# Loading the last 64 rows of w_down as 128 half rows on all partitions, in a one-core attention and FFN decode kernel

## The chip, the core and the metric

The kernel runs on one core of a Trainium2 chip. The metric is device time in microseconds (us). The core has a matmul engine (PE), a vector engine (DVE), an activation engine (ACT), a general engine (POOL), a sequencer that issues transfers (SP), and 16 DMA engines that move data from device memory (HBM) into on-chip memory (SBUF), which has 128 partitions. PE accumulates in PSUM.

## The reference

One token goes through layer norm, then through attention over a cache of 32,768 positions (32 heads of 128) and through a SwiGLU feed-forward block. Both results are added to the input.

```
xn = layernorm(x)                                  # 1 x 640
q  = xn @ wq ; p = softmax(q k^T / sqrt(128)) ; o = p v        # 32 heads, k and v: 32768 x 128 each, bf16
A  = o @ wo                                        # wo: 4096 x 640
B  = (silu(xn @ w_gate) * (xn @ w_up)) @ w_down    # w_gate, w_up: 640 x 1728 ; w_down: 1728 x 640
out = x + A + B
```

The hidden size 1728 is 13 x 128 + 64. These last 64 rows of `w_down` are what the change is about.

## The kernel before

All big loads go through one ring of three slots and are issued by SP, in order: `wq`, then keys and values head by head, then the FFN weights in one slot, then `w_o` in another. Below is the part of SP's program for the FFN and `w_o` (D = 640, F = 1728, FM = 13, FL = 64, NCD = 5).

```
wd = flat[:, d0:d0 + FB * D].rearrange("p (j d) -> p j d", j=FB)
# ... SP:
e.dma_start(wg, B_w_gate.rearrange("(p c) n -> p (c n)", c=NCD)).then_inc(s_ffn[0], 16)
e.dma_start(wu, B_w_up.rearrange("(p c) n -> p (c n)", c=NCD)).then_inc(s_ffn[1], 16)
e.dma_start(flat[:, d0:d0 + FM * D], B_w_down[0:FM * 128, :].rearrange(
    "(p j) n -> p (j n)", j=FM)).then_inc(s_ffn[2], 16)
e.dma_start(wd[0:FL, FM, :], B_w_down[FM * 128:F, :]).then_inc(s_ffn[2], 16)   # 64 rows, 64 partitions
# ... then w_o in six pieces of 8, 8, 8, 5, 2 and 1 rows per partition
```

PE computes gate and up as columns of 128 hidden values, the fourteenth column with 64; DVE and ACT apply the activation; PE multiplies by `w_down` and `w_o` into one accumulator.

```
for j in range(FB):                                   # gate, then up
    n = 128 if j < FM else FL
    for c in range(NCD):
        mm = t.matmul(ffn[0:n, i * FB + j:i * FB + j + 1], lhsT=hidden(w, c, j), rhs=xn[:, c:c + 1], ...)
# ... down:
for j in range(FB):
    n = 128 if j < FM else FL
    for c in range(NCD):
        t.matmul(acc[:, c:c + 1], lhsT=wd_v[0:n, j, c, :], rhs=hcol[0:n, j:j + 1], ...)
# ... DVE: every FFN step twice, for 128 partitions x 13 columns and for 64 partitions x 1 column
```

## Time and profile before

| | before |
|---|---|
| median of the runs | 1288.67 us |
| span of the profiled run | 1286.8 us |
| DMA, mean over the span | 431 GB/s |
| PE, DVE, ACT busy | 81%, 52%, 4% |

The page of the kernel before gives the busy time of each engine and, in 40 equal slices of the span, the busy share of the DMA engines in tenths and their rate:

```profile
span 1286.8 us, 9861 instructions
...
PE 1044.2 (81%) x5153; PEld 261.3 (20%) x3234; DVE 670.3 (52%) x409; ACT 52.2 (4%) x140; POOL 2.5 (0%) x17
...
DMA  9999999999999999999999999999999999999998
GB/s 422 426 424 449 426 430 441 430 434 428 440 428 432 444 428 432 440 430 434 428 440 428 432 444 428 432 440 428 434 428 442 428 432 444 428 432 440 428 418 358
...
```

The DMA row is 9, which means 90% or more, in 39 of 40 slices. PE and DVE have idle time. So the kernel lasts as long as its DMA queue.

The chain of waits of the same run, in order of time (start in us, duration, what), is followed back from the last instruction:

```profile
...
1253.62 29.08 DMA ring<-in_A_wo_dram
...
1282.75 1.49 PE ps L402 x40
...
1284.36 0.17 DVE outb L592
...
1284.88 0.28 DVE orow L594
```

The last 800 KB piece of `w_o` lands 29.08 us after its issue, at 1282.70 us; 40 matmuls and the finish follow. The timeline of the same run (start, duration, engine, operation, and in brackets the idle time before and what ended it) shows whether PE has slack before that:

```profile
...
1274.31 2.10 PE L392 MATMUL ps<-hcol,ring 128*128 128x1 bf16 x70 [1.49 <-DVE hcol L586]
...
1276.34 2.58 PE L402 MATMUL ps<-ot,ring 128*128 128x1 bf16 x80
...
1280.77 1.45 PE L402 MATMUL ps<-ot,ring 128*128 128x1 bf16 x40 [1.84 <-DMA ring<-in_A_wo_dram]
...
1282.75 1.47 PE L402 MATMUL ps<-ot,ring 128*128 128x1 bf16 x40 [0.53 <-DMA ring<-in_A_wo_dram]
...
```

L392 is down, L402 is the product with `w_o`. PE stands idle for 1.84 and 0.53 us until `w_o` pieces land. Work that is moved about on PE before this point does not move the end.

The list of issues by size gives the median time from issue to landing, last on the line:

```profile
...
ring<-in_A_wo_dram SPq DMA_DIRECT2D x3, 1280.0 KB, 25.0
...
ring<-in_A_wo_dram SPq DMA_DIRECT2D x1, 800.0 KB, 29.1
...
ring<-in_A_wo_dram SPq DMA_DIRECT2D x1, 160.0 KB, 28.9
ring<-in_B_w_down_dram SPq DMA_DIRECT2D x1, 80.0 KB, 32.6
...
```

All of them wait most of these 25 to 33 us in the queue: at 424 GB/s, 1280 KB are only 3.1 us. The 80 KB line is the 64-row load: 1239.0 us (its issue in the timeline) + 32.6 = 1271.6 us. Now the table of stretches of the same run, 3 us each (stretch, its length, busy time of each engine and instruction count, granted PE clock, DMA busy share, GB/s):

```profile
...
core 0: us, PE busy (x) PEld busy (x) DVE busy (x) ACT busy (x) POOL busy (x), PEclk, DMA share, GB/s
1266.00:1269.00 3.00, 2.62 (x42) 2.59 (x43) 0.00 (x0) 0.20 (x1) 0.00 (x0) 0.50 1.08 432
1269.00:1272.00 3.00, 3.00 (x53) 3.00 (x53) 0.00 (x0) 0.00 (x0) 0.00 (x0) 0.50 0.93 325
1272.00:1275.00 3.00, 1.51 (x39) 1.44 (x39) 0.93 (x8) 0.23 (x2) 0.00 (x0) 0.50 1.00 420
1275.00:1278.00 3.00, 2.87 (x101) 2.76 (x99) 0.00 (x0) 0.00 (x0) 0.00 (x0) 0.50 1.02 427
...
```

The DMA busy share stays near 1 (0.93 to 1.08), but the rate is 325 GB/s in the stretch in which the 64 rows are served, against 420 to 432 around it. The engines are busy and yet move a quarter less.

The raw packet records say which packets these are. For the same run (start in us on the record's own clock, whose zero lies 11.1 us before the span's start; duration; bytes), when the first of the 64 rows are served:

```
1279.725 0.792 16640
1279.834 0.542 10240
1279.903 0.812 16640
1280.054 0.606 10240
```

Before and after this stretch a packet of 16,640 B takes 0.62 us and one of 10,240 B 0.386 us. The 64 packets of 1280 B themselves mostly take 55 ns (76 ns at most), as do those of the last `w_o` piece. So the transfer looks harmless in its own record; its neighbours are slowed. Strung together by start and duration, the packets of this run form 16 sequences, as many as there are DMA engines, and every sequence has slowed packets in this stretch: 59 packets in all (16,640 B over 0.68 us, 10,240 B over 0.43 us), two to five in each sequence.

### The profile page before, as it was taken

The numbers are of one execution on the slowest core, as the hardware profiler recorded it, in microseconds if no ns is written. First come the engines' busy times: TensorE is split into PE (matmuls) and PEld (weight loads), VectorE is DVE, ScalarE is ACT, GpSimd is POOL, SyncE is SP. The second block draws the span as 40 slices with busy tenths as digits, with TensorE's granted clock in tenths as the row PEclk, the third lists the DMA queues.
The fourth block names the chain that finished last, engine by engine and source line by source line (L and its number), as shares of the span: only waits on it lengthen the run. The fifth ranks groups of instructions, "written<-read, shape, count | busy, mean of one in ns | idle before, by whom it ended". The sixth has DMA issues, their size and how long they took to land.

```text
span 1286.8 us, 9861 instructions
## 1 busy us (share of the span) xinstructions
PE 1044.2 (81%) x5153; PEld 261.3 (20%) x3234; DVE 670.3 (52%) x409; ACT 52.2 (4%) x140; POOL 2.5 (0%) x17
## 2 busy tenths in 40 slices
PE   4599778789777888778798777798777798778797
PEld 1011112221112221112221112221112221112227
DVE  0855665445664446664446664446664446654440
ACT  2000000000000000000000000000000000000000
POOL 0000000000000000000000000000000000000000
PEclk9799888898888998888898888998888998888995
DMA  9999999999999999999999999999999999999998
GB/s 422 426 424 449 426 430 441 430 434 428 440 428 432 444 428 432 440 430 434 428 440 428 432 444 428 432 440 428 434 428 442 428 432 444 428 432 440 428 418 358
DMA packets 11192, 554.17 MB, mean 431 GB/s; under 512 B 1259, under 2 KB 1452, under 8 KB 1708
## 3 DMA queue, kind: packets, MB, share of 16 engines
q1 hardware_dynamic: 11178, 554.00, 99.7%
q8 instruction: 9, 0.15, 0.0%
q14 instruction: 3, 0.02, 0.0%
q10 hardware_dynamic: 2, 0.00, 0.0%
HBM read 553.99 MB, written 0.00 MB: 431 GB/s over the span
## 4 chain that ended last, share of the span: by engine, by line
DMA 53%; PE 30%; DVE 11%; issue 6%; SPq 0%; DVEq 0%
DMA ring<-in_A_k_cache_dram 51%; PE ps L315 17%; PE ps L283 11%; DVE ring L532 10%; DMA ring<-in_A_wo_dram 2%; PE ps L302 1%; PE ps L357 0%; PE ps L351 0%; PE ps L345 0%; PE ps L402 0%; SPq L227 0%; DVEq L532 0%; DVE sc L538 0%; DVE pmax L544 0%; SPq L203 0%
## 5 line engine op out<-in xcount | busy, mean ns | idle before, releaser
L532 DVE TENSOR_TENSOR ring<-ring,qb 128x8192 bf16<-128x8192 bf16 x128 | 557.8, 4420 | 315.6 <-DMA ring<-in_A_k_cache_dram 315.6
L283 PE MATMUL ps<-ring,ident 128*128 128x512 bf16 x1920 | 500.0, 419 | 0.0
L315 PE MATMUL ps<-ring,P 128*4 128x512 bf16 x1984 | 443.3, 379 | 0.0
L302 PE MATMUL ps<-ring,ident 128*128 128x512 bf16 x128 | 55.9, 437 | 217.8 <-DVE ring L532 217.6
L315 PEld LDWEIGHTS ps<-ring,P 128*4 128x4 bf16 x1984 | 163.4, 85 | 237.8
L302 PEld LDWEIGHTS ps<-ring,ident 128*128 128x128 bf16 x128 | 12.6, 99 | 616.9 <-DVE ring L532 343.6
L538 DVE TENSOR_REDUCE sc<-ps 128x64 f32<-128x512 f32 x128 | 82.2, 683 | 63.5 <-PE ps L283 63.5
L550 DVE TENSOR_SCALAR negb<-ps 128x1 f32<-128x1 f32 x32 | 5.1, 158 | 108.4 <-PE ps L357 108.4
L455 ACT ACTIVATE P<-sc,negb 128x256 bf16<-128x256 f32 x32 | 16.2, 507 | 956.5 <-DVE negb L550 956.5
L547 DVE TENSOR_REDUCE m<-ps 1x1 f32<-1x128 f32 x32 | 8.9, 278 | 85.2 <-PE ps L351 85.2
L337 PEld LDWEIGHTS ps<-identf,o 4*128 4x128 f32 x248 | 30.3, 188 | 13.1 <-issue 13.1
L337 PE MATMUL ps<-identf,o 4*128 4x1 f32 x248 | 32.9, 250 | 0.0
L345 PEld LDWEIGHTS ps<-rsum,ones 128*128 128x128 f32 x64 | 12.1, 190 | 99.9 <-issue 99.0
L446 ACT ACTIVATE o<-ps,rzb 4x512 f32<-4x512 f32 x31 | 21.0, 678 | 6.2 <-PE ps L315 6.2
L275 PE MATMUL ps<-ring 128*128 128x512 bf16 x39 | 11.3, 458 | 11.2 <-DMA ring<-in_A_wq_dram 11.2
L451 ACT ACTIVATE ocol<-ps 128x1 f32 (+1 forms) x31 | 5.4, 173 | 222.0 <-PE ps L337 222.0
L544 DVE TENSOR_REDUCE pmax<-sc 128x1 f32<-128x256 f32 x32 | 13.4, 420 | 0.0
L351 PE MATMUL ps<-identf,pmax 128*1 128x128 f32 x64 | 12.2, 273 | 1.2 <-DVE pmax L544 1.2
L357 PE MATMUL ps<-m,ones 1*128 1x1 f32 x64 | 12.1, 256 | 0.4 <-DVE m L547 0.4
L357 PEld LDWEIGHTS ps<-m,ones 1*128 1x128 f32 x64 | 9.4, 182 | 14.2 <-issue 13.5
L381 PE MATMUL ps<-xn,ring 128*128 128x1 bf16 (+1 forms) x140 | 8.9, 198 | 1.0 <-issue 1.0
L520 DVE RECIPROCAL rzb<-ps 128x1 f32<-128x1 f32 x32 | 5.0, 158 | 8.1 <-PE ps L345 8.1
(62 smaller groups left out, 81.1 us busy)
## 6 DMA issues: line engine op xcount, KB each, us to landing
ring<-in_A_wq_dram SPq DMA_DIRECT2D x1, 5120.0 KB, 15.4
ring<-in_A_v_cache_dram SPq DMA_DIRECT2D x1, 4096.0 KB, 31.8
ring<-in_A_wo_dram SPq DMA_DIRECT2D x3, 1280.0 KB, 25.0
ring<-in_B_w_gate_dram SPq DMA_DIRECT2D x1, 2160.0 KB, 23.0
ring<-in_B_w_up_dram SPq DMA_DIRECT2D x1, 2160.0 KB, 27.7
ring<-in_B_w_down_dram SPq DMA_DIRECT2D x1, 2080.0 KB, 31.8
ring<-in_A_v_cache_dram SPq DMA_DIRECT2D x1, 2048.0 KB, 36.4
ring<-in_A_v_cache_dram SPq DMA_DIRECT2D x2, 1024.0 KB, 39.4
```

The costliest lines, as they stand in the source:

```text
L283: return t.add_instruction(mybir.InstMatmult(start_tensor_calc=False, stop_tensor_calc=stop, tile_size=(128, 128), tile_position=(0, 0), l ...
L302: t.matmul(ob, lhsT=ident[:, :], rhs=src, start=True, stop=False)
L315: mm = t.matmul(O, lhsT=P[:, h % PR, j:j + W], rhs=ring[:, s, j * DH:(j + W) * DH], start=(j == 0), stop=(j + W == NJ))
L337: mm = t.matmul(fold_ps, lhsT=o4[:, m * DH:(m + 1) * DH], rhs=identf[0:W, m:m + 1], start=(m == 0), stop=(m == W - 1))
L345: t.matmul(misc[:, 129:130], lhsT=ones[:, :], rhs=rsum[:, h % SR:h % SR + 1], start=True, stop=True).then_inc(s_z, 1)
L351: t.matmul(misc[0:1, 0:128], lhsT=pmax[:, h % SR:h % SR + 1], rhs=identf[:, :], start=True, stop=True).then_inc(s_t, 1)
L357: t.matmul(misc[:, 128:129], lhsT=ones[0:1, :], rhs=m1[0:1, h % SR:h % SR + 1], start=True, stop=True).then_inc(s_b, 1)
L446: a.activation(out=o4[:, :], in_=O, func=ACTF.Copy, scale=rzb[0:W, h % SR:h % SR + 1]).then_inc(s_o4, 1)
L455: a.activation(out=P[:, h % PR, :], in_=sc[:, :], func=ACTF.Exp, bias=negb[:, h % SR:h % SR + 1], scale=c_scale, accum_out=rsum[:, h % SR: ...
L532: v.tensor_tensor(out=kh, in0=kh, in1=q[:, None, :].to_broadcast([128, HF, DH]), op=ALU.mult).then_inc(s_mul, 1)
L538: v.tensor_reduce(out=sc[:, i * HF:(i + 1) * HF], in_=bank[i].rearrange("p (j e) -> p j e", e=G), axis=AX.X, op=ALU.add).then_inc(s_red, 1)
L544: v.tensor_reduce(out=pmax[:, h % SR:h % SR + 1], in_=sc[:, :], axis=AX.X, op=ALU.max).then_inc(s_max, 1)
```

## The change

The 64 rows become 128 half rows of 320 elements: row f lies on partitions 2f and 2f+1. For this, partitions 2f and 2f+1 both need hidden value f, so DVE copies the last 64 columns of gate and up with every column doubled, PE computes all 128 outputs, and the product is masked by the parity of the partition into two columns, one per half of the output. The intent is a load that uses all partitions, and a simpler set of FFN steps, for a little more work on DVE. The diff, cut to its core:

```diff
-        wd = flat[:, d0:d0 + FB * D].rearrange("p (j d) -> p j d", j=FB)
+        wd = flat[:, d0:d0 + FM * D].rearrange("p (j d) -> p j d", j=FM)
+        wdr = flat[:, d0 + FM * D:d0 + FM * D + D // 2]
...
-                        e.dma_start(wd[0:FL, FM, :], B_w_down[FM * 128:F, :]).then_inc(s_ffn[2], 16)
+                        e.dma_start(wdr, B_w_down[FM * 128:F, :].rearrange(
+                            "f (t n) -> (f t) n", t=2)).then_inc(s_ffn[2], 16)
...
+                    for half in range(2):                                  # PE, down, after columns 0..12
+                        a, b = half * (D // 2), (half + 1) * (D // 2)
+                        for c in range(a // 128, (b + 127) // 128):
+                            m0, m1 = max(a, c * 128), min(b, c * 128 + 128)
+                            t.matmul(acc[m0 - c * 128:m1 - c * 128, c:c + 1], lhsT=wdr[:, m0 - a:m1 - a],
+                                     rhs=hcol[:, FM + half:FM + half + 1],
+                                     start=False, stop=False, skip_group_check=True)
...
+                def twice(i):                                              # DVE
+                    v.wait_ge(s_ffn[i], 16)
+                    v.tensor_copy(out=wt[i].rearrange("p c (f t) -> p c f t", t=2),
+                                  in_=(wg_v, wu_v)[i][:, :, FM * 128:F][:, :, :, None].to_broadcast(
+                                      [128, NCD, FL, 2])).then_inc(s_twice, 1)
...
+                v.tensor_scalar(out=hcol[:, FM:FM + 2], in0=par[:, :], scalar1=sg[:, 0, FM:FB],
+                                scalar2=ffn[:, FB + FM:2 * FB], op0=ALU.mult, op1=ALU.mult).then_inc(s_fd, 1)
```

ACT's two exponentials become one, and DVE's eight FFN steps become four, the mask of parities (`par`) and this masked product.

More of the change, by code (lines that the diff above doesn't have):

```diff
@@ L98, in bass_parallel_sum__gqa_block_cached__swiglu_ffn__decode_kernel @@
         ot = sbt("ot", [128, OC], BF16)
-        hcol = sbt("hcol", [128, FB], BF16)
+        hcol = sbt("hcol", [128, FB + 1], BF16)
+        par = sbt("par", [128, 2], F32)
         sg = sbt("sg", [128, 2, FB], F32)
@@ L131, in bass_parallel_sum__gqa_block_cached__swiglu_ffn__decode_kernel @@
         s_att, s_fin = sem("att"), sem("fin")
+        s_twice = sem("twice")
         s_xr, s_or = sem("xr"), sem("orow")
@@ L147, in bass_parallel_sum__gqa_block_cached__swiglu_ffn__decode_kernel @@
         d0 = f0 + 2 * NCD * F
-        wd = flat[:, d0:d0 + FB * D].rearrange("p (j d) -> p j d", j=FB)
-        assert 2 * NCD * F + FB * D <= CE
+        wd = flat[:, d0:d0 + FM * D].rearrange("p (j d) -> p j d", j=FM)
+        wdr = flat[:, d0 + FM * D:d0 + FM * D + D // 2]
+        assert 2 * NCD * F + FM * D + D // 2 <= CE and 2 * FL == 128 and D % 2 == 0
         wg_v = wg.rearrange("p (c n) -> p c n", c=NCD)
@@ L152, in bass_parallel_sum__gqa_block_cached__swiglu_ffn__decode_kernel, with hidden @@
         wd_v = wd.rearrange("p j (c m) -> p j c m", c=NCD)
-        def hidden(w, c, j):
+        u0 = d0 + FM * D + D // 2
+        wt = [flat[:, u0 + i * NCD * 128:u0 + (i + 1) * NCD * 128].rearrange("p (c m) -> p c m", c=NCD)
+              for i in range(2)]
+        assert u0 + 2 * NCD * 128 <= f0 + CE
+        def hidden(i, c, j):
+            w = (wg_v, wu_v)[i]
             if j < FM:
                 return w[:, c, 0:FM * 128].rearrange("p (m j) -> p m j", j=FM)[:, :, j]
-            return w[:, c, FM * 128:F]
+            return wt[i][:, c, :]
         wo = flat[:, WO_S * CE:WO_S * CE + OC * D]
@@ L376, in hidden_part @@
                     t.wait_ge(s_ffn[i], 16)
-                    w = (wg_v, wu_v)[i]
                     for j in range(FB):
-                        n = 128 if j < FM else FL
+                        if j == FM:
+                            t.wait_ge(s_twice, i + 1)
                         for c in range(NCD):
-                            mm = t.matmul(ffn[0:n, i * FB + j:i * FB + j + 1], lhsT=hidden(w, c, j),
+                            mm = t.matmul(ffn[:, i * FB + j:i * FB + j + 1], lhsT=hidden(i, c, j),
                                           rhs=xn[:, c:c + 1], start=(c == 0), stop=(c == NCD - 1))
@@ L386, in down @@
                     t.wait_ge(s_ffn[2], 32)
-                    t.wait_ge(s_fd, 8)
-                    first = True
-                    for j in range(FB):
-                        n = 128 if j < FM else FL
+                    t.wait_ge(s_fd, 6)
+                    for j in range(FM):
                         for c in range(NCD):
-                            t.matmul(acc[:, c:c + 1], lhsT=wd_v[0:n, j, c, :], rhs=hcol[0:n, j:j + 1],
-                                     start=first, stop=False, skip_group_check=True)
-                            first = False
+                            t.matmul(acc[:, c:c + 1], lhsT=wd_v[:, j, c, :], rhs=hcol[:, j:j + 1],
+                                     start=(j == 0 and c == 0), stop=False, skip_group_check=True)
+                    for half in range(2):
[5 more added lines that the diff above has]
+                                     start=False, stop=False, skip_group_check=True)
                 def project():
@@ L478, in act @@
                 a.wait_ge(s_f, 1)
-                a.activation(out=sg[:, 0, 0:FB - 1], in_=ffn[:, 0:FB - 1], func=ACTF.Exp,
-                             scale=-1.0).then_inc(s_fa, 1)
-                a.activation(out=sg[0:FL, 0, FB - 1:FB], in_=ffn[0:FL, FB - 1:FB], func=ACTF.Exp,
-                             scale=-1.0).then_inc(s_fa, 1)
+                a.activation(out=sg[:, 0, :], in_=ffn[:, 0:FB], func=ACTF.Exp, scale=-1.0).then_inc(s_fa, 1)
             @block.vector
@@ L562, in dve @@
                 rz(H - 1)
+                def twice(i):
[3 more added lines that the diff above has]
+                                      [128, NCD, FL, 2])).then_inc(s_twice, 1)
+                twice(0)
                 h = H - 1
@@ L571, in dve @@
                                 in1=blk[:, None, :].to_broadcast([128, H, RB]), op=ALU.mult).then_inc(s_ob, 1)
-                v.wait_ge(s_fa, 2)
-                pieces = [(slice(0, 128), slice(0, FM)), (slice(0, FL), slice(FM, FB))]
-                n = 0
-                for stage in range(4):
-                    for p, f in pieces:
-                        fu = slice(FB + f.start, FB + f.stop)
-                        if stage == 0:
-                            ins = v.tensor_scalar(out=sg[p, 0, f], in0=sg[p, 0, f], scalar1=1.0, scalar2=None,
-                                                  op0=ALU.add)
-                        elif stage == 1:
-                            ins = v.reciprocal(out=sg[p, 1, f], in_=sg[p, 0, f])
-                        elif stage == 2:
-                            ins = v.tensor_tensor(out=sg[p, 0, f], in0=sg[p, 1, f], in1=ffn[p, f], op=ALU.mult)
-                        else:
-                            ins = v.tensor_tensor(out=hcol[p, f], in0=sg[p, 0, f], in1=ffn[p, fu], op=ALU.mult)
-                        ins.then_inc(s_fd, 1)
-                        n += 1
-                    v.wait_ge(s_fd, n)
+                twice(1)
+                v.tensor_reduce(out=par[:, :], in_=ident[:, :].rearrange("p (f t) -> p t f", t=2),
+                                axis=AX.X, op=ALU.add).then_inc(s_fd, 1)
+                v.wait_ge(s_fa, 1)
+                v.tensor_scalar(out=sg[:, 0, :], in0=sg[:, 0, :], scalar1=1.0, scalar2=None,
+                                op0=ALU.add).then_inc(s_fd, 1)
+                v.wait_ge(s_fd, 2)
+                v.reciprocal(out=sg[:, 1, :], in_=sg[:, 0, :]).then_inc(s_fd, 1)
+                v.wait_ge(s_fd, 3)
+                v.tensor_tensor(out=sg[:, 0, :], in0=sg[:, 1, :], in1=ffn[:, 0:FB], op=ALU.mult).then_inc(s_fd, 1)
+                v.wait_ge(s_fd, 4)
+                v.tensor_tensor(out=hcol[:, 0:FM], in0=sg[:, 0, 0:FM], in1=ffn[:, FB:FB + FM],
+                                op=ALU.mult).then_inc(s_fd, 1)
+                v.tensor_scalar(out=hcol[:, FM:FM + 2], in0=par[:, :], scalar1=sg[:, 0, FM:FB],
+                                scalar2=ffn[:, FB + FM:2 * FB], op0=ALU.mult, op1=ALU.mult).then_inc(s_fd, 1)
                 v.wait_ge(s_xr, 1)
```

## The prediction

> **What bounds the kernel now.** DMA, from end to end. The page's slice row shows the 16 DMA engines 90% or more busy in 39 of 40 slices, and its DMA line a mean of 431 GB/s; PE is busy 81%, DVE 52%. The timeline of the last 30 us shows the same for the stage that the change touches: PE is through gate, up and down by 1276.3 us, then stands idle for w_o pieces (0.2, 1.9 and 0.6 us before three groups of its matmuls). The chain of waits ends in a w_o transfer of 29 us, its matmuls, and about 1 us of finish. The queue is served in order: gate, up, down, the 64 last rows, w_o. What counts is when w_o's last byte lands.
>
> **What the change removes.** The 64-row transfer is only 80 KB, 0.19 us at 430 GB/s. But the table of stretches shows the DMA rate falling while it is served: 420 GB/s in 1272-1275 us and 427 in 1275-1278, but 325 in 1269-1272, around its landing at 1239.0 + 32.6 = 1271.6 us. Single packet records agree: its 64 packets of 1280 B take 55 ns each[...], and in those 2.5 us the neighbours' packets slow down (16,640 B from 0.62 to 0.81 us, 10,240 B from 0.386 to 0.54-0.61 us). The 1280 B packets of the last w_o piece, over 128 partitions, do not do this. The summed shortfall is 0.5 to 0.7 us of the whole queue. [...]
>
> **What it adds.** DMA: 128 packets of 640 B, eight an engine; from 55, 102, 244 and 386 ns for 1280 to 10,240 B I estimate 31 ns each, about 0.02 us more per engine. DVE: two copies of 640 elements, estimated at 0.4 to 0.8 us each (the 128x640 broadcast copy near the start took 0.82 us). The first fits between gate's landing (about 1260.7) and 1263.0; the second follows 1265.7, before PE reaches column 14 (about 1272). PE: as many hidden matmuls, 71 instead of 70 in down. ACT one instruction for two, DVE six FFN steps for eight: the 1.5 us gap before down shrinks by some 0.3 us. All this lies before PE's 2.7 us of idle time, so none of it moves the end.
>
> **Critical path.** Only the DMA dip is on it. If it goes altogether, the end comes 0.5 us or more earlier[...]. I expect 0.5 us, 0.04%.
>
> **Predicted time:** 1288.2 us, 80% range 1287.4 to 1289.0. Faster by over 2%: 0.005; within 2%: 0.985; slower by over 2%: 0.01.
>
> **What would show it.** Right: 1269-1272 us holds 400 GB/s or more; w_o pieces land about 0.5 us sooner after issue; PE still ends with waits for w_o; DVE copies under 0.9 us that no one waits for; PE's gap before down near 1.2 us. Wrong: the dip stays[...]; PE waits at the last gate or up column; the last w_o matmuls no longer wait for DMA.
>
> **What would make it wrong.** 640 B packets disturbing neighbours as much; instruction fetches (16 KB, about 1.1 us on one DMA engine) falling on an engine that finishes last[...]; run-to-run steps of 0.5 us, as large as the effect.

The forecast's sum is one term: 0.5 us off the 1288.67 us measured before, which gives the 1288.2 us. That is the low end of the shortfall of 0.5 to 0.7 us in the DMA rate, which the trace shows. "Eight an engine" is 128 packets over 16 engines, a mean; no record names the engine of a packet. "Served in order" rests on the landings: gate at 1260.7 us, up at 1265.7, down at 1270.3, the 64 rows at 1271.6, the pieces of `w_o` after them. An instruction fetch of 16 KB takes 0.99 to 1.13 us in the packet records of the kernel before.

## The result and the profile after

The kernel after takes 1288.09 us (median of 4 runs, 1288.06 to 1288.20), the kernel before 1288.67 us in the same rounds (1288.64 to 1289.19): 0.58 us less, 0.05%. The measured ratio is 0.9995 with a 95% interval of 0.9977 to 1.0012. Ratios are computed as the mean time of one kernel's runs over that of the other's of the same rounds, so they are not quite the ratio of the medians quoted. The interval is wide beside the effect, but the runs are not: all 4 runs after lie below all runs before, by 0.44 us or more. The experiments below rest on such gaps and on the DMA rate in the profile.

The page of the kernel after:

```profile
span 1286.2 us, 9862 instructions
...
PE 1042.2 (81%) x5154; PEld 261.0 (20%) x3235; DVE 672.2 (52%) x409; ACT 52.2 (4%) x139; POOL 2.5 (0%) x17
...
DMA  9999999999999999999999999999999999999998
GB/s 422 426 424 447 429 428 437 436 428 430 444 428 432 442 430 428 428 446 426 432 444 428 430 434 438 428 430 444 428 432 438 432 430 428 444 428 432 444 411 365
...
```

Nothing stands out at this resolution; only the span is 0.6 us shorter. The chain of waits:

```profile
...
1253.85 28.33 DMA ring<-in_A_wo_dram
...
1282.23 1.46 PE ps L416 x40
...
1283.78 0.17 DVE outb L608
...
1284.30 0.28 DVE orow L610
```

The 800 KB piece was issued 0.23 us later than before (1253.85 against 1253.62), took 28.33 instead of 29.08 us, and so landed 0.52 us sooner, at 1282.18 us. What follows it is as long as before, within 0.06 us. The list of issues says the same of every piece of `w_o`, 0.7 to 0.8 us less from issue to landing:

```profile
...
ring<-in_A_wo_dram SPq DMA_DIRECT2D x3, 1280.0 KB, 24.2
...
ring<-in_A_wo_dram SPq DMA_DIRECT2D x1, 800.0 KB, 28.3
...
ring<-in_A_wo_dram SPq DMA_DIRECT2D x1, 160.0 KB, 28.2
ring<-in_B_w_down_dram SPq DMA_DIRECT2D x1, 80.0 KB, 31.7
...
```

The table of stretches shows where this comes from:

```profile
...
1266.00:1269.00 3.00, 2.25 (x41) 2.25 (x42) 0.82 (x2) 0.20 (x1) 0.00 (x0) 0.50 1.03 436
1269.00:1272.00 3.00, 3.00 (x53) 3.00 (x53) 0.00 (x0) 0.00 (x0) 0.00 (x0) 0.50 1.00 406
1272.00:1275.00 3.00, 1.54 (x48) 1.48 (x48) 0.96 (x5) 0.18 (x1) 0.00 (x0) 0.50 0.98 413
1275.00:1278.00 3.00, 3.00 (x112) 2.97 (x109) 0.00 (x0) 0.00 (x0) 0.00 (x0) 0.50 1.01 427
...
```

In 1269-1272 us the rate is now 406 GB/s instead of 325; 81 GB/s over 3 us is 243 KB, or 0.57 us of the queue at 424 GB/s. That is as much as the whole gain. In the packet records of this stretch the 10,240 B packets stay at 0.385 to 0.394 us (but for one of 0.88 us; the kernel before has one too), and the 640 B packets take 32 ns. The timeline of the added and moved work:

```profile
...
1260.69 0.82 DVE L577 COPY ring<-ring 128x640 bf16<-128x640 bf16 x1 [6.69 <-DMA ring<-in_B_w_gate_dram]
...
1265.81 0.82 DVE L577 COPY ring<-ring 128x640 bf16<-128x640 bf16 x1 [2.34 <-DMA ring<-in_B_w_up_dram]
...
1274.11 1.87 PE L400 MATMUL ps<-hcol,ring 128*128 128x1 bf16 x65 [1.46 <-DVE hcol L604]
...
1280.38 1.40 PE L416 MATMUL ps<-ot,ring 128*128 128x1 bf16 x40 [1.92 <-DMA ring<-in_A_wo_dram]
...
1282.23 1.44 PE L416 MATMUL ps<-ot,ring 128*128 128x1 bf16 x40 [0.46 <-DMA ring<-in_A_wo_dram]
...
```

The two copies take 0.82 us each, and no instruction waits for either. Down (L400) is held for 1.46 us before it starts, against 1.49 us before, and PE still waits for `w_o` at the end (L416).

A measure used below is the *loss* of a profiled run: the sum over half microseconds, from 1277 to 1287 us on the record's clock (to 1289 for the run with 320 KB), of how far the DMA rate in the packet records (each packet's bytes spread evenly over its duration) falls short of 424 GB/s, expressed in us of queue time. It is 0.58 us before and 0.04 us after. It comes from one profiled run of each kernel.

### The profile page after: what moved, and what is told of

It is laid out like the page before. It is cut to its first block, busy times and chain, and to the rows that moved or that the text cites. A ratio compares the mean times of both kernels' runs of the same rounds, so it can differ in the third digit from the quotient of the medians.

```text
span 1286.2 us, 9862 instructions
## 1 busy us (share of the span) xinstructions
PE 1042.2 (81%) x5154; PEld 261.0 (20%) x3235; DVE 672.2 (52%) x409; ACT 52.2 (4%) x139; POOL 2.5 (0%) x17
## 4 chain that ended last, share of the span: by engine, by line
DMA 53%; PE 29%; DVE 12%; issue 5%; SPq 0%; DVEq 0%
DMA ring<-in_A_k_cache_dram 51%; PE ps L325 17%; DVE ring L543 12%; PE ps L293 10%; DMA ring<-in_A_wo_dram 2%; PE ps L312 1%; PE ps L367 0%; PE ps L361 0%; PE ps L355 0%; PE ps L416 0%; SPq L237 0%; DVEq L543 0%; DVE sc L549 0%; DVE pmax L555 0%; SPq L212 0%
## 5 line engine op out<-in xcount | busy, mean ns | idle before, releaser
L391 PE MATMUL ps<-xn,ring 128*128 128x1 bf16 x140 | 8.4, 196 | 1.6 <-issue 1.6
```

## The experiments

Theory A, which the prediction favoured: the whole gain is the vanished dip in the DMA rate. Rival B: the shorter steps on ACT and DVE. Twelve runs were made, all with 5 timed rounds beside the kernel before, in four groups, each group on another chip; the kernel before had medians of 1288.73, 1288.81, 1288.86 and 1288.62 us in them. Differences below are to the kernel before of the same group.

### 1. The load alone, and the arithmetic alone

The kernel before, with the new load only. The arithmetic then reads wrong values:

```diff
-e.dma_start(wd[0:FL, FM, :], B_w_down[FM * 128:F, :]).then_inc(s_ffn[2], 16)
+e.dma_start(flat[:, d0 + FM * D:d0 + FM * D + D // 2], B_w_down[FM * 128:F, :].rearrange(
+    "f (t n) -> (f t) n", t=2)).then_inc(s_ffn[2], 16)
```

> The kernel before with only the transfer of the change: the 64 rows come as 128 half rows on all partitions, the arithmetic stays as before and so reads wrong values (wrong on purpose). Theory A (the dip in the DMA rate while 64 rows go to 64 partitions is the whole gain): the dip goes, about 1288.1 us, as the kernel after. Rival B (the gain comes from the shorter FFN steps on ACT and DVE): the time stays at about 1288.7 us.

Measured: 1288.16 us, 0.57 less than before, loss 0.05 us. The result was wrong, as meant. The stretch of the dip in its table of stretches:

```profile
...
1269.00:1272.00 3.00, 3.00 (x53) 3.00 (x53) 0.00 (x0) 0.20 (x1) 0.00 (x0) 0.50 1.02 415
...
```

The other half of the square: the kernel after, with the old load. Half of the partitions then multiply with leftover data:

```diff
-e.dma_start(wdr, B_w_down[FM * 128:F, :].rearrange("f (t n) -> (f t) n", t=2)).then_inc(s_ffn[2], 16)
+e.dma_start(flat[0:FL, d0 + FM * D:d0 + FM * D + D], B_w_down[FM * 128:F, :]).then_inc(s_ffn[2], 16)
-        u0 = d0 + FM * D + D // 2
+        u0 = d0 + FM * D + D
```

> The kernel after with the old transfer: 64 full rows to partitions 0..63, all added arithmetic kept (wrong on purpose, since the second half of the partitions holds other data). Theory A: the dip is back, about 1288.7 us, as the kernel before, and the added copies cost nothing. Rival B: about 1288.1 us. If the copies cost something that the load hides, this is over 1288.8 us.

Measured: 1288.66 us, 0.07 less than before and within its scatter (1288.52 to 1288.84), loss 0.60 us; wrong, as meant. The same stretch:

```profile
...
1269.00:1272.00 3.00, 3.00 (x54) 3.00 (x53) 0.00 (x0) 0.00 (x0) 0.00 (x0) 0.50 0.90 319
...
```

The load alone gives the gain (0.57 of 0.58 us) and removes the dip; the arithmetic alone gives nothing and keeps it. Rival B is out.

### 2. The same bytes once more, in both forms

Could any 80 KB from one small region of HBM, or any run of short packets, make the dip? Both runs add to the kernel after a second copy of the 64 rows, unused, right behind the first (`last` is `B_w_down[FM * 128:F, :]`, `e0` a free place in the slot). Only the form differs:

```diff
+e.dma_start(flat[:, e0:e0 + D // 2], last.rearrange("f (t n) -> (f t) n", t=2)).then_inc(s_x2, 16)   # x128
+e.dma_start(flat[0:64, e0:e0 + D], last).then_inc(s_x2, 16)                                          # x64
```

> The kernel after with a second, unused copy of the same 80 KB as 128 half rows, right behind the first. Theory A: only its bytes cost: 8 packets of 32 ns an engine, so +0.2 to 0.3 us over the kernel after (1288.3 to 1288.4 us), no dip. Theory C (any 80 KB read from one contiguous stretch of HBM, or any short packets, disturb the queue): +0.6 us or more and a dip.

> The kernel after with a second, unused copy of the same 80 KB as 64 full rows on partitions 0..63, right behind the half rows. Same bytes and same source as the run with the half rows twice. Theory A: a dip as in the kernel before, +0.7 to 0.9 us over the kernel after (1288.8 to 1289.0 us). Theory C: the same time as with the half rows twice.

Measured: 1288.41 us for half rows twice (loss 0.07), 1289.08 us with 64 full rows (loss 0.57). The stretch of each, half rows first:

```profile
...
1269.00:1272.00 3.00, 3.00 (x56) 3.00 (x54) 0.00 (x0) 0.00 (x0) 0.00 (x0) 0.50 1.01 404
...
```

```profile
...
1269.00:1272.00 3.00, 3.00 (x53) 3.00 (x53) 0.00 (x0) 0.00 (x0) 0.00 (x0) 0.50 1.00 337
...
```

Same source, same bytes, same place in the queue: 0.67 us apart. The bytes alone cost about 0.3 us over the kernel after. It is the destination or the packet size, not the source.

### 3. Packet size, and how many partitions

Four more forms of the extra 80 KB (the edits are cut to the transfers). "One packet per engine" is 16 packets over 16 engines, a mean:

```diff
+e.dma_start(flat[0:64, e0:e0 + 800].rearrange("p (t n) -> p t n", t=2)[:, :, 0:D // 2],             # x64half
+            last.rearrange("f (t n) -> f t n", t=2)).then_inc(s_x2, 16)
+e.dma_start(flat[0:32, e0:e0 + 2 * D], last.rearrange("(p r) n -> p (r n)", r=2))...                 # x32
+e.dma_start(flat[0:16, e0:e0 + 4 * D], last.rearrange("(p r) n -> p (r n)", r=4))...                 # x16
+e.dma_start(flat[0:32, e0:e0 + D], last[0:32, :])... ; e.dma_start(flat[64:96, e0:e0 + D], last[32:64, :])...   # x32x2
```

> The kernel after with an extra, unused 80 KB as in the run with 64 extra rows, but each row as two packets of 640 B, so that only the 64 partitions are left of it and the packet size is that of the half rows. Theory A1 (the number of partitions[...] makes the dip): as with 64 full rows, 1288.8 to 1289.3 us, with the dip. Theory R (the packet size makes it): as with half rows on all partitions, 1288.3 to 1288.5 us, no dip.

> Extra, unused 80 KB on partitions 0..31 as 2560 B packets. [...] as with 64 partitions, 1288.8 to 1289.3 us. If the number of partitions counts by itself (half as many): the dip cost doubles from 0.67 to about 1.3 us, near 1289.7 us. If longer packets cure it: 1288.4 us.

> Extra, unused 80 KB on partitions 0..15, one 5120 B packet per engine. [...] near 1290.4 us, and surely over 1289.6 us. [...] near 1289.0 us or less.

> Extra, unused 80 KB as two transfers of 32 rows each, one to partitions 0..31 and one to 64..95: the same rows and packets as with 64 rows[...]. [...] no dip, 1288.4 to 1288.6 us. If it is what all engines do at the moment: a dip as with 64 rows, 1288.9 to 1289.3 us.

| extra 80 KB | packets | us | to before | loss, us |
|---|---|---|---|---|
| partitions 0..127 (section 2) | 640 B | 1288.41 | -0.32 | 0.07 |
| 0..63 (section 2) | 1280 B | 1289.08 | +0.35 | 0.57 |
| 0..63, two packets a row | 640 B | 1289.06 | +0.25 | 0.67 |
| 0..31 | 2560 B | 1288.82 | +0.01 | 0.62 |
| 0..15 | 5120 B | 1289.04 | +0.23 | 0.65 |
| 0..31, then 64..95 | 1280 B | 1288.74 | -0.07 | 0.33 |

The same stretch of these four, in the order of the table (packets of 640 B, 0..31, 0..15, two transfers):

```profile
...
1269.00:1272.00 3.00, 3.00 (x54) 3.00 (x52) 0.00 (x0) 0.00 (x0) 0.00 (x0) 0.50 1.00 325
...
```

```profile
...
1269.00:1272.00 3.00, 3.00 (x53) 3.00 (x53) 0.00 (x0) 0.00 (x0) 0.00 (x0) 0.50 0.97 328
...
```

```profile
...
1269.00:1272.00 3.00, 3.00 (x53) 3.00 (x52) 0.00 (x0) 0.00 (x0) 0.00 (x0) 0.50 0.97 317
...
```

```profile
...
1269.00:1272.00 3.00, 3.00 (x53) 3.00 (x53) 0.00 (x0) 0.00 (x0) 0.00 (x0) 0.50 0.98 358
...
```

Packet size is out: 640 B packets on 64 partitions make the full dip, and packets of 2560 and 5120 B do not cure it. The expectation for 16 partitions failed: about 1290.4 us was expected, and 1289.04 us was measured, as in its other branch (near 1289.0 us or less). The same 80 KB lost 0.57 us on 64 partitions, 0.62 us on 32 and 0.65 us on 16: within the lower half the number of partitions hardly changes the loss of these 80 KB. The run on 0..31 has the full loss in the records, yet a median time 0.2 to 0.3 us below those of the other one-sided runs in the table. The profiled executions, from which the losses come, do not differ so: 1288.86 us on 0..31 against 1288.85, 1288.91 and 1288.91 us. The gap lies in executions without a profile and is not explained.

What 0..15, 0..31 and 0..63 have in common is that they lie in the lower half of the partitions. Two transfers of 32 rows, one in each half, lost 0.33 us, about half, and their time, 1288.74 us, lies between the two expectations (1288.4 to 1288.6 us without a dip, 1288.9 to 1289.3 us with one). Why it is about half is not shown.

### 4. Another window of 64 partitions

The single transfers to fewer than 128 partitions so far all began at partition 0. Two more runs move the window of 64 partitions and keep rows and packets: 32..95 has 32 partitions in each half, 64..127 is the upper half. A third writes four times the bytes to 0..63. Theory H is that the dip goes by which partitions are written, so that 32..95 has none and 64..127 has one.

```diff
+e.dma_start(flat[32:96, e0:e0 + D], last).then_inc(s_x2, 16)      # x64mid
+e.dma_start(flat[64:128, e0:e0 + D], last).then_inc(s_x2, 16)     # x64hi
+e.dma_start(flat[0:64, e0:e0 + 4 * D], B_w_down[F - 256:F, :].rearrange("(p r) n -> p (r n)", r=4)).then_inc(s_x2, 16)   # x64d4
```

> Extra, unused 80 KB as 64 full rows on partitions 32..95. [...] Theory H[...]: no dip, 1288.3 to 1288.5 us as with half rows. Theory N (fewer than 128 partitions is enough, whichever): dip, 1288.8 to 1289.2 us.

> Extra, unused 80 KB as 64 full rows on partitions 64..127[...]. Theory H and theory N: dip as on 0..63, 1288.8 to 1289.2 us. If it is special to partitions 0..63, which hold something else: no dip, 1288.4 us.

> Extra, unused 320 KB on partitions 0..63: four times the bytes, one transfer, rows of 5120 B. The bytes alone cost 0.77 us at 424 GB/s over the kernel after. Theory D (the loss goes by bytes, 0.6 us per 80 KB): 2.4 us more, near 1291.3 us. Theory M (the whole queue is slowed as long as any one engine is in such a transfer; the engines pass it over 2.2 us, so 0.6 us longer engine time each makes the slow stretch only 1.3 times as long): loss 0.8 us, near 1289.7 us.

Measured: 1288.59 us on 32..95 (0.27 less than before, loss 0.05); 1288.96 us on 64..127 (0.10 more, loss 0.54); 1292.59 us with 320 KB on 0..63 (3.73 more, loss 2.03). Their stretches, in this order:

```profile
...
1269.00:1272.00 3.00, 3.00 (x54) 3.00 (x53) 0.00 (x0) 0.00 (x0) 0.00 (x0) 0.50 0.99 402
...
```

```profile
...
1269.00:1272.00 3.00, 3.00 (x53) 3.00 (x52) 0.00 (x0) 0.00 (x0) 0.00 (x0) 0.50 1.00 341
...
```

```profile
...
1269.00:1272.00 3.00, 3.00 (x53) 3.00 (x52) 0.00 (x0) 0.00 (x0) 0.00 (x0) 0.50 1.02 218
1272.00:1275.00 3.00, 1.54 (x51) 1.48 (x51) 0.96 (x5) 0.18 (x1) 0.00 (x0) 0.50 0.97 328
...
```

The run on 32..95 decides. Its transfer has 64 partitions, 1280 B packets, and the same source and bytes as the one to 0..63; it has no dip (402 GB/s in the stretch, loss 0.05 us), and in its packet records no sequence has a slowed packet. (Its time is 0.09 us over the range expected, that of the run on 0..63 0.08 us.) So "fewer than 128 partitions" is not the cause; it matters which partitions are written. The upper half alone is about as bad as the lower (0.54 against 0.57 us). So the pattern in these runs is: a transfer of 80 KB that lies in one half of the partitions loses 0.54 to 0.67 us, one that lies evenly in both 0.04 to 0.07 us, and two one-sided transfers, one for each half, lose 0.33 us together. What in the chip makes this pattern is not shown: no run tells one mechanism from another.

With four times the bytes the rate falls to 218 GB/s, about half of the usual, for a whole stretch. Why it is half is not shown. Theory M of the expectation (a fixed slow stretch, about 1289.7 us) is out; theory D (by bytes) gave 1291.3 us, and even that was 1.3 us too low. Of the 4.5 us over the kernel after, by the medians, 0.77 us are bytes and 2.03 us are loss in the records; 1.7 us are left. The profiled run was one of the two quickest of the five (1292.03 us), which accounts for 0.56 us of it. The packet records show where the other 1.2 us lie: one of the sequences of packets finishes late. Its last eight packets of `w_o` are alone in the record and end at 1286.88 us of the span, against 1282.91 us for the last packet in the kernel after, 4.0 us later, while the point at which 300 KB are still to come is only 2.8 us later. Why it is late is not known.

### 5. A kernel made from this

If it is enough to write 32..95, the doubled arithmetic is not needed. This kernel, made from the one before, puts the 64 full rows on partitions 32..95. The last gate and up column is computed for 96 columns instead of 64, so that the last 64 hidden values come out on partitions 32..95 (the other 32 are repeats that nothing uses); the other partitions of that hidden column are zero, and down uses all 128 partitions, where the unused ones multiply zero with finite leftover data of the slot. The diff is cut to its core:

```diff
-e.dma_start(wd[0:FL, FM, :], B_w_down[FM * 128:F, :]).then_inc(s_ffn[2], 16)
+e.dma_start(wd[32:96, FM, :], B_w_down[FM * 128:F, :]).then_inc(s_ffn[2], 16)
-            return w[:, c, FM * 128:F]
+            return w[:, c, FM * 128 - 32:F]
-                        n = 128 if j < FM else FL
+                        n = 128 if j < FM else FL + 32                       # hidden part
-                            t.matmul(acc[:, c:c + 1], lhsT=wd_v[0:n, j, c, :], rhs=hcol[0:n, j:j + 1],
+                            t.matmul(acc[:, c:c + 1], lhsT=wd_v[:, j, c, :], rhs=hcol[:, j:j + 1],
+                done(g.memset(hcol[:, :], 0.0))                                # POOL, at the start
+                # DVE: hcol[0:128, 0:13], hcol[32:64, 13:14] and hcol[64:96, 13:14], three products
```

> A correct kernel made from the one before, without half rows and without computing anything twice: the 64 rows of down go as full rows to partitions 32..95, the last gate and up columns are computed for 96 columns so that they come out on partitions 32..95, and the other partitions of that hidden column are zero. Theory H: no dip, 1288.0 to 1288.2 us, the same as the kernel after to within 0.1 us. Theory N (the unused copy in the run on 32..95 was harmless for another reason): dip, 1288.7 us.

Measured: correct, 1288.23 us (1288.09 to 1288.41), 0.39 less than before in its group, loss 0.04 us:

```profile
...
1269.00:1272.00 3.00, 3.00 (x53) 3.00 (x53) 0.00 (x0) 0.13 (x1) 0.00 (x0) 0.50 0.97 396
...
```

The dip is gone without half rows and doubled columns. The time is 0.14 us above the median of the kernel after, from another group; the expectation of "within 0.1 us" was missed by a little. Each against the kernel before of its own rounds, it gains 0.39 us and the kernel after 0.58 us. Two of its five runs took about 1288.4 us, the others 1288.1 to 1288.2; what makes the two apart was not looked for. So this is a simpler kernel that keeps most of the gain, not one that beats the kernel after.

## Why the prediction was right

- *DMA bounds the kernel, and only the end of the queue counts*: right. The arithmetic alone (section 1) moved the time by 0.07 us.
- *The dip of 0.5 to 0.7 us around the 64-row transfer goes*: right. 325 became 406 GB/s, the loss went from 0.58 to 0.04 us, and the time fell by 0.58 us, where the prediction chose 0.5 and gave 1288.2 us.
- *The cause of the dip*: what the runs show is that it matters which partitions are written: 32..95 has no dip (loss 0.05 us) with as many partitions as 0..63 (0.57 us). Fewer partitions in the lower half did hardly more harm: 16 lost 0.65 us. Why is open (section 4).
- *The whole dip rather than part of it*: no part stayed. The prediction had a smaller figure beside the full dip. The prediction hedged here and gave no reason for choosing the full dip; that its number came within 0.1 us is luck to that extent. By the packet records of the kernel before all 16 sequences have slowed packets, while the 64 packets, 3.7 us of packet time in a stretch of 2.3 us, keep 1.6 sequences at a time busy on average; why was not tried.
- *640 B packets take 31 ns*: measured 32 ns. *They might disturb neighbours as much*: they do not on 128 partitions (loss 0.04 us, and 0.07 us with them twice), and do on 64 (0.67 us).
- *DVE copies of 0.4 to 0.8 us that no one waits for*: 0.82 us each, just above the range; no one waited.
- *The gap before down shrinks by 0.3 us, to about 1.2*: wrong, 1.46 against 1.49 us. The steps are fewer, but each pair of steps before took 0.22 to 0.25 us together in the timeline, the single ones now take 0.17 to 0.24 us, and the masked product takes 0.29 us. The wrong size cost nothing, being off the critical path.

## What to carry to other kernels

In a kernel bound by DMA, look for stretches in which the DMA engines are fully busy and the rate falls: a transfer can look cheap in its own record and be paid for by its neighbours' packets (here packets of 55 ns, and 0.58 us lost beside them). For a load of 64 rows it is worth trying the middle (here 32..95) instead of 0..63 or 64..127; here that was worth 0.6 us for 80 KB between the two unused copies, and 0.39 us in the correct kernel, without half rows. Arithmetic that ended before PE's last wait for DMA was free here (0.07 us less with all of the added work, within the scatter), so neither its cost nor its saving should be counted.
